# Turning part of q and x by DMA instead of on TensorE, with two batches of loads held behind these turns and batch 2's work scheduled four slots later

## Chip, cores, metric

One core of one Trainium2 chip. The metric is the device time of one execution in microseconds (us). Engine names are those of the profile: PE is TensorE, DVE is VectorE, ACT is ScalarE, POOL is GpSimd, SP is SyncE (it only issues DMA here; "SPq" is its queue).

## The reference, cut

```python
kv  = einsum('bhsd,bhse->bhde', k, v)             # 8 batches, 8 heads, 576 rows, 64 wide
out = einsum('bhsd,bhde->bhse', q, kv)
out = out / sqrt(mean(out*out, -1) + 1e-6) * g_norm
x   = out.transpose(0, 2, 1, 3).reshape(8, 576, 512)
xn  = (x - mean) / sqrt(var + 1e-6) * g_ln
return x + relu(xn @ w_ch1) @ w_ch2               # 512 -> 2048 -> 512
```

## The kernel before

The two large matrix products (the MLP) form one stream on TensorE. Its unit here is the **slot**: one group of matmuls, 0.86 to 0.89 us. Each batch takes 32 slots, 16 for the first product (mm1) and 16 for the second (mm2): slots 32 and 48 start mm1 and mm2 of batch 1, 64 and 80 those of batch 2, slot 96 mm1 of batch 3. The attention of later batches is put between the slots by an agenda. `at(slot, fn)` runs fn, that is, emits its instructions, just before that slot. In this kernel batch 4's q had landed by 101.8 us (87.9 + 13.9), and DVE copied it only at 106.18, after the tile work emitted ahead of it; SP sent an x turn that was ready at 106.26 only at 110.22, behind a q turn.

```python
def load_batch(b, after=None):
    if after is not None:
        nc.gpsimd.tensor_copy(gate, after)   # L98: the loads are issued behind this one-element copy
    load(k_in[b % NB], k, b)                 # two buffers each of k, v, q
    load(v_in[b % NB], v, b)
    load(q_in[b % NB], q, b)
...
def turn_q_dma(b):
    nc.vector.tensor_copy(q_p ..., q_in[b % NB])              # L202, DVE
    nc.sync.dma_start_transpose(q_t ..., q_p ...)             # L204, SP, 20 blocks of 128x128
...
def kv_of(b):
    kv_ps = ps_m.tile(..., tag="misc")       # K^T V, L245; ps_m has ONE buffer
...
class Tile:                                  # 128 rows of x
    o()    # q times KV on PE (L270), into ps_out, two buffers
    sq()   # ACT      red()  # DVE
    y()    # DVE L302 x()    # DVE L321     xc()  # DVE L331
    def turn(self, on_pe):
        if on_pe:
            tp = ps_m.tile(..., tag="misc")                   # the same single buffer
            ... four PE transposes (L347), then an ACT copy (L349)
        else:
            nc.sync.dma_start_transpose(dst, self.xc_t)       # L351, SP, four blocks
...
def plan_tile(s, make, turn_at, on_pe):
    at(s, o, sq, red);  at(s + 2, y, x, xc);  at(s + 6, var);  at(turn_at, turn)
...
q_turns(23, 1)        # batch 1's q: five turns on PE (L170), slots 23 to 26.5
for j, s, tn in ((0, 24, 30), (1, 27, 34), (2, 31, 38), (3, 35, 42)):
    plan_tile(s, lambda j=j: main_tile(1, j), tn, True)
at(36, lambda: kv_of(2))
at(36.5, lambda: turn_q_dma(2))
for j, s, tn in ((0, 44, 50), (1, 48, 54), (2, 53, 61), (3, 58, 67)):
    plan_tile(s, lambda j=j: main_tile(2, j), tn, j > 1)      # two tiles turned by DMA, two on PE
plan_tile(62, lambda: rem_tile(1), 69, False)                 # the 64 rows left over of batches 0 and 1
for b in range(3, B):
    s = 32 * b
    at(47 if b == 3 else s - 60,
       lambda b=b: load_batch(b, qts[b - 1][:1, J, HP - 1, 127:]))
    d = -41 if b == 3 else -45
    at(s + d, lambda b=b: kv_of(b));  at(s + d + 1.7, lambda b=b: turn_q_dma(b))
    for j in range(J):
        o = s + d + (10 if b == 3 else 13) + 5 * j
        plan_tile(o, lambda b=b, j=j: main_tile(b, j), o + 6, False)
    if b % 2:
        plan_tile(s - 14, lambda b=b: rem_tile(b), s - 8, False)
```

Slot 96 (mm1 of batch 3) needs all four x tiles of batch 3 turned, and its neighbour in the stream needs batch 4's q turned. Both are DMA transposes on SP.

## Time and profile before

| | before |
|---|---|
| time, median of 3 runs | 290.87 us (290.82 to 290.95) |
| span of the profiled run | 289.2 us |
| granted TensorE clock | 1.00 |
| PE idle from 30 us to slot 96 | 0.9 us of 83.2 |

The page of the kernel before, parts 1, 2 and 4 (busy time and share of each engine; busy tenths and granted clock in 40 slices; the chain of work that ended last):

```profile
PE 279.8 (97%) x2289; PEld 158.9 (55%) x2315; DVE 149.8 (52%) x331; ACT 155.4 (54%) x338; POOL 40.9 (14%) x68
PE   7889999999999999999999999999999999999995
PEclk9999999999999999999999999999999999999999
PE 91%; DMA 2%; DVE 2%; ACT 2%; issue 1%; DVEq 0%; POOLq 0%
```

TensorE bounds the kernel: busy everywhere, full clock, and the chain of waits is almost all PE. So I took every stall put into its stream to lengthen the kernel.

The timeline of POOL's gate copies before (start, duration, engine, line, operation; in brackets the idle time ahead of it and what ended it), for the loads of batches 3 and 4:

```profile
61.90 0.18 POOL L98 COPY gate<-qt 1x1 bf16<-1x1 bf16 x1 [23.43 <-DMA qt<-q_p]
83.38 0.18 POOL L98 COPY gate<-qt 1x1 bf16<-1x1 bf16 x1 [16.93 <-DMA qt<-q_p]
```

So a batch's loads begin when the q turn of the batch before has landed: a late q turn makes the next batch's loads late, and so its K^T V and its q turn.

The timeline of the kernel before, selected lines of DVE, SP and PE near slot 96:

```profile
105.51 0.75 DVE L331 SCALAR_TENSOR_TENSOR xc<-x_blk,st_blk,g_ln_sb 128x512 bf16<-128x512 f32 x1
106.18 0.82 DVE L202 COPY q_p<-q_in 128x2560 bf16<-128x2560 bf16 x1
107.06 3.11 SPq L204 DMA_TRANSPOSE qt<-q_p  x1
110.22 1.26 SPq L351 DMA_TRANSPOSE xT_blk<-xc  x1
112.66 0.39 PE L270 MATMUL o_ps<-kv_pack,qt 128*128 128x128 bf16 x4
112.88 1.89 PE L412 MATMUL p<-xT_blk,w_sb 128*128 128x512 bf16 x8
```

Batch 4's q turn goes out at 107.06 and batch 3's last x turn behind it at 110.22. The latter took 2.5 us to land (tile view), so it landed at about 112.7, and slot 96 starts at 112.88 without a stall. There is about 0.2 us of slack. (The tile itself was ready at 106.26, so its turn stood 4.0 us behind the q turn here too, and cost nothing.)

### The profile page before, as it was taken

The numbers are of one execution on the slowest core, as the hardware profiler recorded it, in microseconds if no ns is written. First come the engines' busy times: TensorE is split into PE (matmuls) and PEld (weight loads), VectorE is DVE, ScalarE is ACT, GpSimd is POOL, SyncE is SP. The second block draws the span as 40 slices with busy tenths as digits, with TensorE's granted clock in tenths as the row PEclk, the third lists the DMA queues.
The fourth block names the chain that finished last, engine by engine and source line by source line (L and its number), as shares of the span: only waits on it lengthen the run. The fifth ranks groups of instructions, "written<-read, shape, count | busy, mean of one in ns | idle before, by whom it ended". The sixth has DMA issues, their size and how long they took to land.

```text
span 289.2 us, 5765 instructions
## 1 busy us (share of the span) xinstructions
PE 279.8 (97%) x2289; PEld 158.9 (55%) x2315; DVE 149.8 (52%) x331; ACT 155.4 (54%) x338; POOL 40.9 (14%) x68
## 2 busy tenths in 40 slices
PE   7889999999999999999999999999999999999995
PEld 3579755995569644445444444444444444444444
DVE  5774028838987783765366925762578300220022
ACT  3477854985469832882288418920894076016500
POOL 8522520031032003200410022000000000000000
PEclk9999999999999999999999999999999999999999
DMA  7999999569999929996997179937202510131033
GB/s 215 199 208 202 201 203 206 125 103 196 151 168 129 178 53 165 184 164 123 144 211 102 39 146 204 170 79 161 54 18 54 111 36 0 39 82 27 0 74 73
DMA packets 64890, 36.10 MB, mean 125 GB/s; under 512 B 32860, under 2 KB 59868, under 8 KB 64864
## 3 DMA queue, kind: packets, MB, share of 16 engines
q0 software_dynamic: 28528, 17.76, 46.0%
q1 hardware_dynamic: 35824, 17.25, 31.3%
q10 hardware_dynamic: 512, 0.72, 0.7%
q8 instruction: 18, 0.29, 0.4%
q14 instruction: 8, 0.07, 0.1%
HBM read 36.71 MB, written 9.44 MB: 160 GB/s over the span
## 4 chain that ended last, share of the span: by engine, by line
PE 91%; DMA 2%; DVE 2%; ACT 2%; issue 1%; DVEq 0%; POOLq 0%
PE p L428 43%; PE p L412 42%; PE o_ps L270 3%; DMA v_in<-in_v_dram 2%; PE kv_ps L245 2%; ACT m L415 1%; DVE x_blk L288 0%; DVE xc L546 0%; PE tp L347 0%; ACT sq L276 0%; ACT xT_blk L349 0%; PE tp L170 0%; ACT rms L307 0%; DVE ss L512 0%; PE tp L553 0%
## 5 line engine op out<-in xcount | busy, mean ns | idle before, releaser
L412 PE MATMUL p<-xT_blk,w_sb 128*128 128x128 bf16 (+2 forms) x1017 | 131.4, 285 | 0.8
L428 PE MATMUL p<-w_sb,m 128*128 128x512 bf16 (+2 forms) x590 | 126.8, 368 | 1.6 <-issue 1.0
L415 ACT ACTIVATE m<-p 128x512 bf16<-128x512 f32 x144 | 85.4, 596 | 43.9 <-PE p L412 41.8
L412 PEld LDWEIGHTS <-w_sb 128*128 128x128 bf16 x1024 | 78.6, 98 | 44.5 <-issue 1.1
L428 PEld LDWEIGHTS <-m 128*128 128x128 bf16 x608 | 56.8, 98 | 61.7
L433 DVE SCALAR_TENSOR_TENSOR o_sb<-p,rstd,x_blk 128x512 f32<-128x512 f32 (+2 forms) x38 | 27.3, 721 | 53.2 <-PE p L428 47.6
L276 ACT ACTIVATE sq<-o_ps 128x512 f32<-128x512 f32 x35 | 20.9, 596 | 42.1 <-PE o_ps L270 42.1
L297 DVE TENSOR_REDUCE ss<-sq 128x8 f32<-128x512 f32 x35 | 23.7, 678 | 11.4 <-ACT sq L276 11.4
L339 ACT ACTIVATE dev<-x_blk,st_blk 128x512 f32<-128x512 f32 x36 | 25.7, 714 | 4.6 <-DVE st_blk L325 4.4
L331 DVE SCALAR_TENSOR_TENSOR xc<-x_blk,st_blk,g_ln_sb 128x512 bf16<-128x512 f32 x34 | 25.6, 752 | 1.2
L302 DVE TENSOR_TENSOR y<-o_ps,inv 128x512 f32<-128x512 f32 x33 | 22.8, 692 | 3.0
L321 DVE SCALAR_TENSOR_TENSOR x_blk<-y,g_norm_sb 128x512 f32<-128x512 f32 x33 | 22.8, 692 | 1.1
L314 DVE RECIPROCAL inv<-rms 128x8 f32<-128x8 f32 x36 | 7.2, 201 | 24.8 <-ACT rms L307 24.8
L421 DVE RECIPROCAL rstd<-rstd 128x4 f32<-128x4 f32 x9 | 1.6, 174 | 34.7 <-ACT rstd L420 34.7
L98 POOL COPY gate<-qt 1x1 bf16<-1x1 bf16 x5 | 0.9, 176 | 113.2 <-DMA qt<-q_p 113.2
L307 ACT ACTIVATE rms<-ss,eps_sb 128x8 f32<-128x8 f32 x36 | 10.7, 297 | 8.0 <-DVE ss L297 7.7
L270 PEld LDWEIGHTS <-qt 128*128 128x128 bf16 (+1 forms) x156 | 10.2, 100 | 7.3 <-issue 1.7
L270 PE MATMUL o_ps<-kv_pack,qt 128*128 128x128 bf16 (+1 forms) x156 | 13.7, 220 | 0.1
L197 PE MATMUL p<-fill_sb 128*128 128x512 bf16 x26 | 7.8, 449 | 1.3 <-DVE eps_sb L137 1.2
L339 ACT ACTIVATION_READ_ACCUMULATOR dev<-x_blk,st_blk 128x1 f32 x36 | 6.9, 190 | 0.0
L248 ACT CAST kv_pack<-kv_ps 64x256 bf16<-64x256 f32 x7 | 2.6, 365 | 7.2 <-PE kv_ps L245 7.2
L245 PEld LDWEIGHTS <-k_in 128*64 128x64 bf16 x280 | 5.0, 112 | 2.6 <-issue 2.5
(79 smaller groups left out, 116.5 us busy)
## 6 DMA issues: line engine op xcount, KB each, us to landing
out_dram<-o_sb SPq DMA_DIRECT2D x70, 128.0 KB, 2.4
w_sb<-in_moe_w_ch_dram POOLq DMA_DIRECT2D x8, 512.0 KB, 14.0
k_in<-in_k_dram POOLq DMA_DIRECT2D x7, 320.0 KB, 5.8
v_in<-in_v_dram POOLq DMA_DIRECT2D x7, 320.0 KB, 10.2
q_in<-in_q_dram POOLq DMA_DIRECT2D x7, 320.0 KB, 13.0
q_in<-in_q_dram POOLq DMA_DIRECT2D x8, 256.0 KB, 13.3
k_in<-in_k_dram POOLq DMA_DIRECT2D x7, 256.0 KB, 7.4
v_in<-in_v_dram POOLq DMA_DIRECT2D x7, 256.0 KB, 11.0
```

The costliest lines, as they stand in the source:

```text
L245: nc.tensor.matmul(kv_ps[hh * D:hh * D + D, hp, :], lhsT=k_in[b % NB][:, h, j, :], rhs=v_in[b % NB][:, h, j, :], start=(j == 0), stop=(j = ...
L270: nc.tensor.matmul(flat[rows, hp * 128:(hp + 1) * 128], lhsT=lhsT_of(hp), rhs=kvp[:, hp, :], start=True, stop=True)
L276: nc.scalar.activation(self.sq_t, self.o_ps, func=AF.Square)
L297: nc.vector.tensor_reduce(self.ss, self.sq_t, axis=AX.X, op=ALU.add)
L302: nc.vector.tensor_mul(self.y_t, self.o_ps, self.inv().to_broadcast([128, H, D]))
L321: nc.vector.scalar_tensor_tensor(x_blk[:, ts].rearrange("p (h d) -> p h d", h=H), in0=self.y_t, scalar=1.0, in1=g_norm_sb.to_broadcast([12 ...
L331: nc.vector.scalar_tensor_tensor(self.xc_t, in0=x_blk[:, self.ts], scalar=st[:, 1, self.ts:self.ts + 1], in1=g_ln_sb, op0=ALU.add, op1=ALU ...
L339: nc.scalar.activation(dev, x_blk[:, ts], func=AF.Square, bias=st[:, 1, ts:ts + 1], accum_out=st[:, 2, ts:ts + 1])
L412: nc.tensor.matmul(p1[:, i, :], lhsT=w1_sb[:, kk, de * 128:(de + 1) * 128], rhs=blk[2][:, kk, sl], start=(kk == 0), stop=(kk == nK - 1))
L415: nc.scalar.activation(m1[:, de0:de0 + per, sl], p1, func=AF.Relu)
L428: nc.tensor.matmul(p2[:, c0:c1], lhsT=m1s[b][:, de, ts * 128:(ts + 1) * 128], rhs=w2_sb[:, de, c0:c1], start=(de == 0), stop=(de == nDe - 1))
L433: nc.vector.scalar_tensor_tensor(o_sb[:, c0:c1], in0=p2[:, c0:c1], scalar=rstds[b][:, ts:ts + 1], in1=blks[b][0][:, ts, c0:c1], op0=ALU.mu ...
```

## The change

Its intent is to take 20 transposes of 128x128 blocks off the engine that bounds: three of batch 1's five q turns (12 blocks) and two x tiles of batch 2 (8 blocks) go to DMA transposes on SP. So that these do not run beside loads, batch 2's loads are held behind batch 1's q turn, and batch 4's behind an x turn of batch 2 as well as batch 3's q turn. Since batch 2's loads come later, its work is moved on.

```diff
-    def load_batch(b, after=None):
-        if after is not None:
-            nc.gpsimd.tensor_copy(gate, after)
+    def load_batch(b, *after):
+        for element in after:
+            nc.gpsimd.tensor_copy(gate, element)
... (next_loads)
-        load_batch(2)
+        load_batch(2, qts[1][:1, J, HP - 1, 127:])
...
-    at(9.5, next_loads)
... (q_turns)
+            q_p = q_ps.pop(b)
+            nc.sync.dma_start_transpose(
+                qts[b][:, 2:].rearrange("p j hp t -> p (j hp) t"),
+                q_p[:, 2:].rearrange("p j h d -> p (j h d)"))
-        for i, j in enumerate((2, 3, 4)):
-            at(s + 1.5 + i, lambda j=j: turn_q(b, j, ps_m, "misc"))
-        at(s + 4, lambda: q_ps.pop(b))
...
+    at(24, next_loads)
...
-    at(36, lambda: kv_of(2))
-    at(36.5, lambda: turn_q_dma(2))
-    for j, s, tn in ((0, 44, 50), (1, 48, 54), (2, 53, 61), (3, 58, 67)):
-        plan_tile(s, lambda j=j: main_tile(2, j), tn, j > 1)
-    plan_tile(62, lambda: rem_tile(1), 69, False)
+    at(38.5, lambda: kv_of(2))
+    at(41.5, lambda: turn_q_dma(2))
+    for j, s, tn in ((0, 48, 54), (1, 52, 58), (2, 56, 62), (3, 60, 66)):
+        plan_tile(s, lambda j=j: main_tile(2, j), tn, False)
+    plan_tile(70, lambda: rem_tile(1), 76, False)
...
-           lambda b=b: load_batch(b, qts[b - 1][:1, J, HP - 1, 127:]))
-        d = -41 if b == 3 else -45
+           lambda b=b: load_batch(b, qts[b - 1][:1, J, HP - 1, 127:],
+                                  *([blks[2][2][:1, nK - 1, 511:]] if b == 4 else [])))
+        d = -39 if b == 3 else -45
```

All of batch 3's attention comes two slots later (d from -41 to -39).

## The prediction

> **What bounds it now.** TensorE. The page's first part has PE busy 279.8 of 289.2 us (97%), at a granted clock of full speed in every slice; the chain of waits is 91% PE (two matmul lines 43% and 42%). After 18 us the chain has almost no gap. Time falls only by PE work removed, and rises by stalls put into PE's stream.
>
> **What the change removes.** Twelve PE transposes of batch 1's q (three of five turns) and eight of batch 2's x (two of its tiles). In the chain a full turn of four costs 0.22 us and the half turn about 0.16: 0.6 + 0.44 = about 1.0 us of PE, all of it on the critical path. Five ACT copies go too; ACT is not the bound, so they save nothing by themselves.
>
> **What it adds.** One DMA transpose of 12 blocks and two more of 4. Twenty blocks take 3.2 us of SP issue and land after 5.1 us (DMA view). The copy of q ends at 38.2 us, so I expect the 12 blocks to land at 42.5 to 44.
>
> **What it moves.** Batch 2's loads, issued from 30.3 us before, now wait for that landing and start near 43 to 44.5. A batch's six loads need (batch 3, timeline and DMA view) 9.3 us from first issue until v has landed and 13.1 until q has. Then batch 2: v 53 to 55, wanted by PE near 55.3 (slot 38); q 57 to 59, wanted by DVE near 58.5. Its q turn lands at about 64.5 (61.9 before), wanted near 65.5. Margins under 2 us, no large stall.
>
> Batch 3's loads follow that landing: first issue about 65.0 (62.4 before). v lands at 74.3 to 74.8; PE wants it at about 73.9: a stall of 0.4 to 0.9 us. Its q turn should land near 84.2, just as wanted.
>
> Batch 2's last x turn goes out on SP behind batch 3's q turn (3.2 us) and stores, landing at about 88 to 90; PE wants it near 89. Batch 4's loads now wait for it: first issue about 88.5 to 90 (84.6 before). There [...] v needed 13 us: 101 to 103, wanted at about 100.5. That stall, 0 to 2.5 us, is the largest risk.
>
> [...] an x turn lands in 2.5 us undisturbed and in 10.4 beside batch 4's loads.
>
> **Sum.** -1.0 of PE work, +0.9 of new stalls in the middle of my estimates: 290.8 us, 8 in 10 between 289.4 and 292.6. Chances: faster by over 2% 0.01, within 2% 0.96, slower by over 2% 0.03.
>
> **What would show it.** PE busy falls by about 1 us. New PE idle time in front of the K^T V matmuls of batches 3 and 4 (waiting for v), none or under 0.5 us at batch 2. The gate copy ahead of batch 2's loads at 43 to 45 us, of batch 3's near 64.5, of batch 4's 88 to 90.
>
> **What would make it wrong.** If 12 blocks land by 42 and loads run as fast as batch 3's, no stall appears and the time is about 289.8. If batch 0's stores slow batch 2's loads by over 2 us, each later batch inherits the delay and the time passes 292.

The x turn's 2.5 and 10.4 us and v's 13 us are measured in the kernel before. The sum is -1.0 + 0.9 = -0.1 us, from 290.9 to 290.8.

## More of the kernel before

The windows view of the kernel before, from 30 us to 0.3 us past the start of slot 96 (length, then busy time and count of each engine, clock, DMA share, GB/s):

```profile
core 0: us, PE busy (x) PEld busy (x) DVE busy (x) ACT busy (x) POOL busy (x), PEclk, DMA share, GB/s
30.00:113.20 83.20, 82.29 (x897) 56.83 (x903) 54.38 (x117) 52.90 (x123) 13.15 (x23) 1.00 1.06 156
```

## The result, and the profile after

| | before | after |
|---|---|---|
| time, median of 4 runs | 290.91 us (290.82 to 291.21) | 301.71 us (300.64 to 302.92) |
| ratio after/before | | 1.037 (1.033 to 1.041): slower |
| span of the profiled run | 289.2 us | 298.5 us |
| PE idle from 30 us to slot 96 | 0.9 us | 9.25 us |

A ratio is the mean time of one kernel's fast runs over that of the other's of the same rounds, so it is not quite the ratio of the medians. The result lies far outside the predicted range. The profiled run of after was its fastest, with a mean granted clock of 0.998; its other runs had 0.994 to 1.000.

The page of the kernel after, the same parts:

```profile
PE 283.1 (95%) x2295; PEld 158.5 (53%) x2295; DVE 150.0 (50%) x331; ACT 153.7 (51%) x333; POOL 41.2 (14%) x70
PE   8999999799789898799999999999999999999994
PEclk9999999999999999999999999999999999999999
PE 65%; DMA 11%; DVE 9%; issue 6%; ACT 4%; SPq 2%; POOL 1%; DVEq 0%; POOLq 0%; ACTq 0%
```

The PE row has dents (7 and 8) from the eighth slice to the nineteenth and none later, and the chain has moved from PE to DMA, DVE and waits. PE's busy time did not fall, but 18 mm2 matmuls (590 against 608) and 7 of mm1 (1017 against 1024) are missing from the records of before, so the busy sums of the two pages are not compared. That the 20 transposes are gone shows in the weight loads, which are complete: PEld x2315 before, x2295 after.

The windows view of the kernel after, from 30 us to 0.3 us past the start of slot 96:

```profile
30.00:122.25 92.25, 83.00 (x886) 56.13 (x884) 55.67 (x118) 51.70 (x118) 15.20 (x27) 1.00 0.94 150
```

The stretch is 9.05 us longer and PE is idle for 8.34 us more of it, at full clock. The two differ by 0.7 us, about what missing records and modelled ends allow. So nearly all of the loss is PE waiting, before slot 96. Where TensorE stood at the slot starts (PE timeline of both):

| start of | slot 48 | slot 64 | slot 80 | slot 96 | end of span |
|---|---|---|---|---|---|
| before | 66.64 | 82.22 | 97.75 | 112.88 | 289.2 |
| after | 67.80 | 84.78 | 102.26 | 121.93 | 298.5 |
| difference | +1.2 | +2.6 | +4.5 | +9.05 | +9.3 |

The last column adds almost nothing: from batch 3's MLP on the two kernels run alike in these two profiled runs. Half of the loss falls between slots 80 and 96.

The PE timeline of the kernel after, its waits of over half a microsecond up to slot 96:

```profile
56.81 0.82 PE L245 MATMUL kv_ps<-v_in,k_in 128*64 128x64 bf16 x40 [1.50 <-ACT xT_blk L349]
...
67.57 0.40 PE L270 MATMUL o_ps<-kv_pack,qt 128*128 128x128 bf16 x4 [0.67 <-DMA qt<-q_p]
...
77.75 0.82 PE L245 MATMUL kv_ps<-v_in,k_in 128*64 128x64 bf16 x40 [1.57 <-DMA v_in<-in_v_dram]
...
88.80 0.40 PE L270 MATMUL o_ps<-kv_pack,qt 128*128 128x128 bf16 x4 [1.24 <-ACT m L415]
...
99.65 2.78 PE L412 MATMUL p<-xT_blk,w_sb 128*128 128x256 bf16 x24 [0.74 <-ACT m L415]
...
104.89 0.41 PE L270 MATMUL o_ps<-kv_pack,qt 128*64 128x128 bf16 x8 [0.52 <-DVE y L302]
...
115.58 3.61 PE L428 MATMUL p<-w_sb,m 128*128 128x512 bf16 x16 [0.68 <-DVE o_sb L433]
...
119.81 0.40 PE L270 MATMUL o_ps<-kv_pack,qt 128*128 128x128 bf16 x4 [0.62 <-DMA qt<-q_p]
...
121.93 4.49 PE L412 MATMUL p<-xT_blk,w_sb 128*128 128x512 bf16 x20 [1.72 <-DMA xT_blk<-xc]
```

They sum to 9.3 us (1.50 + 0.67 + 1.57 + 1.24 + 0.74 + 0.52 + 0.68 + 0.62 + 1.72), nine waits and no large one. Only the third is a load (v of batch 3), and none is v of batch 4, which I had called the largest risk. The first is a wait for a PSUM buffer: batch 2's v had landed at 54.8, but K^T V of batch 2 and the PE turn of batch 1's third x tile now fall in the same slot 38 and share the single "misc" buffer, so that K^T V waits for ACT's copy of the turn. The wait at 88.80 is batch 3's q turn, whose landing released the gate at 88.88: the profile puts PE's wait down to ACT, but the weight load of the same matmul waited 1.52 us for DMA qt<-q_p. The wait at 99.65 is for ScalarE's eviction, which stood in program order behind a small activation (L307 at 98.81) that had waited 1.21 us for VectorE's sum (L297).

POOL's gates of the kernel after, for the loads of batches 2, 3 and 4 (two gates for batch 4):

```profile
43.74 0.18 POOL L98 COPY gate<-qt 1x1 bf16<-1x1 bf16 x1 [13.55 <-DMA qt<-q_p]
67.64 0.18 POOL L98 COPY gate<-qt 1x1 bf16<-1x1 bf16 x1 [19.32 <-DMA qt<-q_p]
88.88 0.18 POOL L98 COPY gate<-qt 1x1 bf16<-1x1 bf16 x1 [16.63 <-DMA qt<-q_p]
93.54 0.18 POOL L98 COPY gate<-xT_blk 1x1 bf16<-1x1 bf16 x1 [4.49 <-DMA xT_blk<-xc]
```

The first is where I put it (43 to 44.5). The second, predicted at 64.5, came at 67.64: VectorE waited 1.44 us for q of batch 2 and copied it at 59.98, and the turn, issued at 60.83, took 6.7 us to land instead of 5.1. The last, predicted for 88 to 90, came at 93.54.

The timeline of the kernel after near slot 96, selected lines of DVE and SP, to be held against the six lines of before:

```profile
110.84 0.75 DVE L331 SCALAR_TENSOR_TENSOR xc<-x_blk,st_blk,g_ln_sb 128x512 bf16<-128x512 f32 x1 [0.30 <-DVE st_blk L325]
...
113.39 0.75 DVE L331 SCALAR_TENSOR_TENSOR xc<-x_blk,st_blk,g_ln_sb 128x512 bf16<-128x512 f32 x1
114.05 0.82 DVE L202 COPY q_p<-q_in 128x2560 bf16<-128x2560 bf16 x1
114.94 3.11 SPq L204 DMA_TRANSPOSE qt<-q_p  x1
118.14 0.54 SPq L446 DMA_DIRECT2D out_dram<-o_sb  x1
118.74 0.59 SPq L447 DMA_DIRECT2D out_dram<-o_sb  x1
119.38 2.60 SPq L351 DMA_TRANSPOSE xT_blk<-xc  x2
```

Batch 3's last x tile was ready at about 111.6 (110.84 + 0.75) but its turn went out at 119.38, behind batch 4's q turn and two stores. It is this turn for which slot 96 waits at 121.93. The q turn itself is late because VectorE came to its copy at 114.05 (106.18 before), behind the work of two x tiles: batch 3's last tile now shares slots 82 and 84 with the remainder tile of batches 2 and 3.

### The profile page after: what moved, and what is told of

Read it like the earlier page. It is cut to its first block, busy times and chain, and to the rows that moved or that the text cites. A ratio compares the mean times of both kernels' runs of the same rounds, so it can differ in the third digit from the quotient of the medians.

```text
span 298.5 us, 5751 instructions
## 1 busy us (share of the span) xinstructions
PE 283.1 (95%) x2295; PEld 158.5 (53%) x2295; DVE 150.0 (50%) x331; ACT 153.7 (51%) x333; POOL 41.2 (14%) x70
## 4 chain that ended last, share of the span: by engine, by line
PE 65%; DMA 11%; DVE 9%; issue 6%; ACT 4%; SPq 2%; POOL 1%; DVEq 0%; POOLq 0%; ACTq 0%
PE p L428 31%; PE p L412 31%; DMA q_in<-in_q_dram 4%; DMA qt<-q_p 2%; PE o_ps L270 2%; DMA out_dram<-o_sb 2%; DMA gn_row<-in_g_norm_dram 2%; ACT m L415 2%; DVE y L302 1%; DVE ss L297 1%; DVE x_blk L321 1%; SPq L204 1%; PE kv_ps L245 1%; ACT rms L307 1%; DVE o_sb L433 1%
## 5 line engine op out<-in xcount | busy, mean ns | idle before, releaser
L428 PE MATMUL p<-w_sb,m 128*128 128x512 bf16 (+2 forms) x608 | 128.9, 368 | 0.7 <-DVE o_sb L433 0.7
L297 DVE TENSOR_REDUCE ss<-sq 128x8 f32<-128x512 f32 x35 | 23.7, 678 | 11.9 <-ACT sq L276 11.9
L331 DVE SCALAR_TENSOR_TENSOR xc<-x_blk,st_blk,g_ln_sb 128x512 bf16<-128x512 f32 x34 | 25.6, 752 | 1.5 <-DVE st_blk L325 0.3
L307 ACT ACTIVATE rms<-ss,eps_sb 128x8 f32<-128x8 f32 x36 | 10.6, 297 | 11.4 <-DVE ss L297 11.3
L197 PE MATMUL p<-fill_sb 128*128 128x512 bf16 x27 | 9.4, 508 | 1.2 <-DVE eps_sb L137 1.2
L245 PE MATMUL kv_ps<-v_in,k_in 128*64 128x64 bf16 x280 | 5.8, 197 | 3.1 <-DMA v_in<-in_v_dram 1.6
```

Of the source, the lines that this page charges most:

```text
L245: nc.tensor.matmul(kv_ps[hh * D:hh * D + D, hp, :], lhsT=k_in[b % NB][:, h, j, :], rhs=v_in[b % NB][:, h, j, :], start=(j == 0), stop=(j = ...
L297: nc.vector.tensor_reduce(self.ss, self.sq_t, axis=AX.X, op=ALU.add)
L331: nc.vector.scalar_tensor_tensor(self.xc_t, in0=x_blk[:, self.ts], scalar=st[:, 1, self.ts:self.ts + 1], in1=g_ln_sb, op0=ALU.add, op1=ALU ...
L428: nc.tensor.matmul(p2[:, c0:c1], lhsT=m1s[b][:, de, ts * 128:(ts + 1) * 128], rhs=w2_sb[:, de, c0:c1], start=(de == 0), stop=(de == nDe - 1))
```

## The experiments

Eighteen kernels ran; all gave correct results. Four timed runs of each (five of the best one).

| label | what | median us | ratio (95%) |
|---|---|---|---|
| r1_no_hold_2 | after, batch 2's loads not held | 302.55 | 1.039 (1.036 to 1.042) |
| r2_no_hold_4 | after, batch 4's second gate away | 309.57 | 1.063 (1.058 to 1.067) |
| r3_hold_2_alone | before, batch 2's loads held | 297.29 | 1.021 (1.016 to 1.027) |
| r4_turns_alone | before, both kinds of DMA turn | 299.69 | 1.028 (1.022 to 1.034) |
| r5_x_turns_alone | before, x turns by DMA | 297.66 | 1.023 (1.022 to 1.025) |
| r6_q_turn_alone | before, q turns by DMA | 291.95 | 1.004 (1.002 to 1.005) |
| r7_x_on_pe | after, x turns back on PE, no second gate | 302.79 | 1.042 (1.039 to 1.045) |
| r8_move_alone | before, only the later slots | 301.61 | 1.036 (1.034 to 1.038) |
| s1_tiles_late_alone | before, batch 2's tiles later | 292.43 | 1.005 (1.004 to 1.007) |
| s2_rem_and_b3_late | before, remainder and batch 3 later | 297.82 | 1.023 (1.021 to 1.025) |
| s3_rem_early | after, remainder tile early | 301.56 | 1.038 (1.034 to 1.041) |
| s5_part | before, 8 q blocks and one x tile by DMA | 290.45 | 0.9987 (0.9974 to 0.9999) |
| t1_b3_late_alone | before, batch 3 two slots later | 296.99 | 1.021 (1.018 to 1.023) |
| t2_rem_late_alone | before, remainder tile later | 293.11 | 1.007 (1.006 to 1.009) |
| t3_b3_tiles_back | after, batch 3's last three tiles at their old slots | 299.15 | 1.028 (1.023 to 1.033) |
| t4_b2_move_alone | before, batch 2 later | 297.54 | 1.024 (1.021 to 1.027) |
| u1_b3_late_turn_first | t1 with the x turn ahead on SP | 292.10 | 1.004 (1.002 to 1.005) |
| u2_after_turn_first | after with the x turn ahead on SP | 300.67 | 1.034 (1.030 to 1.039) |

Before of the same rounds was between 290.88 and 291.01 throughout. Executions of one kernel differ by up to 3.9 us (r4) once PE waits long, and the longer ones mostly have the lower mean clock: r8 took 300.51 us at 1.000 and 301.57 to 301.85 at 0.993 to 0.994, t3 297.74 and 298.03 at 1.000, 300.27 and 300.58 at 0.994. Differences of a microsecond between two such kernels therefore mean little by themselves. The theories at the start were: the holds make loads late (what my prediction feared); the DMA turns themselves land late; the moved slots cost it.

### The holds taken away from the kernel after

```diff
  r1_no_hold_2
-        load_batch(2, qts[1][:1, J, HP - 1, 127:])
+        load_batch(2)
-    at(24, next_loads)
+    at(9.5, next_loads)
  r2_no_hold_4
-                                  *([blks[2][2][:1, nK - 1, 511:]] if b == 4 else [])))
+                                  ))
```

> The changed kernel with batch 2's loads issued at once again (near 30 us), all else as changed. Theory A (the hold puts batch 2's loads, and through the gate copies those of 3 and 4, on one serial chain of load, copy, turn that starts too late): most of the 10.8 us comes back, 290 to 293 us, the gate ahead of batch 3's loads falls from 67.6 to under 64 us, and the idle time of TensorE between 60 and 105 us falls from about 8 us to under 3. Theory B (the second hold of batch 4 behind the x turn is what costs): 299 us or more. Theory C (moving batch 2's work four slots on collides with other work on PSUM and the in-order engines): 298 us or more. Theory D (a turn by DMA beside loads is too slow): 299 us or more, since turns and loads now overlap more.

> The changed kernel without the second gate copy of batch 4. Its loads start at the landing of batch 3's q turn, 88.9 us, instead of 93.5. Theory A: 4.7 us of the chain go, and the stalls after 107 us (about 3 us) with them, nothing before: 297 to 299 us. Theory B: 293 us or less. Theory C: no change, over 300 us.

Neither helped. Without batch 2's hold the time stayed at 302.55 us. The issue of batch 1's q turn, now beside loads, took 3.25 us instead of 1.54 and PE waited 1.99 us for its landing. That wait replaced what the hold had cost, and the two waits of the kernel after for batch 2's q turn (0.67) and batch 3's v (1.57) were gone; the others were there (0.24 to 2.37 us each). So the hold of batch 2's loads alone is not the cause. Without batch 4's second gate the kernel lost another 8 us. The PE timeline of that run, at mm1 of batch 2:

```profile
101.15 6.91 PE L412 MATMUL p<-xT_blk,w_sb 128*128 128x256 bf16 x40 [5.92 <-DMA xT_blk<-xc]
```

An x turn landing beside batch 4's loads made PE wait 5.92 us in one piece. Given the DMA turns, this hold is needed.

### Each part put into the kernel before

r3 adds the hold of batch 2's loads (on an element that the PE turns write last, at slot 27.5), r4 both kinds of DMA turn, r5 and r6 one kind each, r8 only the changed slot numbers.

```diff
  r3_hold_2_alone
-        load_batch(2)
+        load_batch(2, qts[1][:1, J, HP - 1, 63:64])
-    at(9.5, next_loads)
+    at(27.5, next_loads)
  r4_turns_alone: the two lines of r5 and r6 together
  r5_x_turns_alone
-        plan_tile(s, lambda j=j: main_tile(2, j), tn, j > 1)
+        plan_tile(s, lambda j=j: main_tile(2, j), tn, False)
  r6_q_turn_alone: the q_turns part of the change
  r8_move_alone
-    at(36, lambda: kv_of(2)) ... turn_q_dma(2) at 36.5, tiles ((0, 44, 50), (1, 48, 54), (2, 53, 61), (3, 58, 67))
+    at(38.5, lambda: kv_of(2)) ... at 41.5, tiles ((0, 48, 54), (1, 52, 58), (2, 56, 62), (3, 60, 66))
-    plan_tile(62, lambda: rem_tile(1), 69, False)
+    plan_tile(70, lambda: rem_tile(1), 76, False)
-        d = -41 if b == 3 else -45
+        d = -39 if b == 3 else -45
```

> The kernel before with nothing but the hold: batch 2's loads wait until batch 1's last q turn (on TensorE) is copied, about 44.6 us. Theory A: the loss appears without any DMA turn, move or second hold: 296 us or more, with TensorE waiting for v of batch 2 at slot 36 and for later q turns. Theories B, C and D: within 2 us of the kernel before, 291 to 293.

> The kernel before with nothing but the turns by DMA (three fifths of batch 1's q, the last two x tiles of batch 2), no hold, no move. Theory A: the 1.0 us of TensorE work comes off, less a small stall where a turn runs beside batch 2's loads: 289.8 to 291.5 us. Theory D: turns land 8 us or more after issue and stall TensorE at the third tile of batch 1 (near 48 us) and at batch 2's third tile, 293 us or more.

> The kernel before with only the last two x turns of batch 2 by DMA. Theory E (a turn by DMA that goes out beside a batch's loads lands 7 to 12 us after issue, and TensorE stands until it lands[...]): the last x turn meets batch 4's loads, TensorE stands 3 to 4 us at slot 72 and then runs slow for 3 to 5 us: 294 to 297 us, mean clock below 0.99. Theory F (the loss is the later start of the loads, on the serial chain from one batch's q turn to the next batch's loads): nothing moves here, so 290 to 291 us.

> The kernel before with only batch 1's q turn (12 blocks) by DMA. Theory E: it meets batch 2's loads, lands near 50 us, TensorE stands 2 us at the third tile of batch 1 and runs slow after it: 293 to 295 us, with no further stall over 1 us later. Theory F: 290 to 291 us.

> The kernel before with only batch 2's work moved four slots on (and the slots of the remainder tile and of batch 3 with it), no DMA turn, no hold. Theory E: no turn meets loads, so under 292 us. Theory F: the gate of batch 3's loads falls later by 2.5 to 3.5 us (61.9 to about 65), batch 3's q turn with it, and TensorE waits for v of batch 3 and for its q turn: 293 to 295 us. Theory C (a new collision on the single PSUM buffer that x turns and K^T V share: both now stand in slot 38): a stall of 1.5 us at K^T V of batch 2, waiting for ACT's copy, in this run as in the changed kernel.

Every part alone costs time: the hold +6.3 us, the x turns +6.8, the q turn +1.1, both turns +8.7. The move alone costs +10.7, as much as the whole change (+10.8). It has no DMA turn and no hold beyond those of before. So the later slots suffice to lose everything, and with the slots moved the holds and the turns add nothing on balance. That the slots are also necessary is not shown: the change with its holds and turns but with the old slots was not run, and r3 and r4 lose 6.3 and 8.7 us in the old slots.

The PE timeline and then two windows of r4 (both turns in the old slots, no holds):

```profile
50.09 0.40 PE L270 MATMUL o_ps<-kv_pack,qt 128*128 128x128 bf16 x4 [2.08 <-DMA qt<-q_p]
...
96.36 5.30 PE L412 MATMUL p<-xT_blk,w_sb 128*128 128x256 bf16 x24 [3.49 <-DMA xT_blk<-xc]
```

```profile
52.00:54.00 2.00, 2.00 (x22) 2.00 (x21) 0.63 (x1) 0.41 (x1) 0.00 (x0) 0.50 1.23 302
98.00:100.00 2.00, 2.00 (x12) 1.39 (x10) 0.00 (x0) 0.60 (x2) 0.00 (x0) 0.50 1.35 183
```

Two things are to be seen. The turns beside loads land late, 2.08 and 3.49 us after PE wants them. And the granted clock (third column from the right) was 0.50 after each wait: the 24 matmuls after the second took 5.30 us where 24 such matmuls take 2.78 in the kernel after. r5 shows the same with a wait of 4.02 us (0.50 from 94 to 98); r6, with a wait of 1.72, kept the full clock (1.00 from 46 to 54). A wait of about two microseconds thus cost more than its length in some runs and not in others. The PE timelines of r8 and then of r7 at slot 96 show the same wait of 2.44 us, with 6.18 us for the 20 matmuls after it in the first (mean clock of the run 0.994) and 4.49 in the second (0.999):

```profile
122.12 6.18 PE L412 MATMUL p<-xT_blk,w_sb 128*128 128x512 bf16 x20 [2.44 <-DMA xT_blk<-xc]
```

```profile
122.79 4.49 PE L412 MATMUL p<-xT_blk,w_sb 128*128 128x512 bf16 x20 [2.44 <-DMA xT_blk<-xc]
```

The SP queue on batch 1's q turn, in the kernel after (loads held) and then in r4 (loads running):

```profile
38.58 1.54 SPq L612 DMA_TRANSPOSE qt<-q_p  x1
```

```profile
38.24 3.35 SPq L613 DMA_TRANSPOSE qt<-q_p  x1
```

The 12 blocks landed at 43.7 in the first, 5.1 us after issue, and at about 50 in the second, 11.8 us after (PE, which waited for them, went on at 50.09).

r7 asked the opposite question, whether the kernel after recovers if the x turns go back to PE (and the second gate goes, as nothing needs it then):

```diff
  r7_x_on_pe
-        plan_tile(s, lambda j=j: main_tile(2, j), tn, False)
+        plan_tile(s, lambda j=j: main_tile(2, j), tn, j > 1)
  and the second gate of batch 4 away
```

> The changed kernel with batch 2's last two x turns back on TensorE and so without the second hold (batch 4's loads start at the landing of batch 3's q turn). Theory E says the x turn and its hold cost only what the hold delays: the gate of batch 4 falls from 93.5 to about 89 us and the stalls after 98 us (4.3 us in sum) shrink to under 2: 297 to 299 us. Theory F says that stalls before 90 us (5 us) remain in full, which E agrees with for the hold of batch 2. If the x turns were the main part, 294 us or less.

It did not: 302.79 us, with the same late waits (0.74, 0.51, 0.42, 0.61 and 2.44 us). In the kernel after the x turns by DMA are not the cause.

### Which part of the move

```diff
  s1_tiles_late_alone     tiles of batch 2 to ((0, 48, 54), (1, 52, 58), (2, 56, 62), (3, 60, 66))
  s2_rem_and_b3_late      plan_tile(70, rem_tile(1), 76) and d = -39
  s3_rem_early            the kernel after with plan_tile(42, rem_tile(1), 49)
  t1_b3_late_alone        d = -39, nothing else
  t2_rem_late_alone       plan_tile(70, rem_tile(1), 76), nothing else
  t4_b2_move_alone        kv_of(2) at 38.5, turn_q_dma(2) at 41.5, and s1's tiles
```

> The kernel before with only the four tiles of batch 2 moved to the changed kernel's slots (48, 52, 56, 60); K^T V and the q turn of batch 2, the remainder tile and batch 3 stay. Theory G (the move empties VectorE at 60 to 68 us, where it did the first tile or two of batch 2, and this work then queues up behind other work until slot 96, so x of batch 2 and 3 and q_p come late): gates of batches 3 and 4 stay near 62 and 83 us, but TensorE still waits for xc, for evictions and for batch 3's last x: 293 to 297 us. Theory F (the later loads of batch 3 are what costs): no gate moves, so under 292 us.

> The kernel before with only the remainder tile of batches 0 and 1 (slot 62 to 70) and batch 3's work (two slots later) moved. Theory G: VectorE's 3.3 us for the remainder tile now fall among batch 3's tiles, so batch 3's last x and q_p of batch 4 come late: TensorE waits 1 to 2 us at slot 96: 291.5 to 293 us. Theory F: the loads are unchanged, within 0.5 us of the kernel before.

> The changed kernel with the remainder tile of batches 0 and 1 at slot 42 (its turn at 49), that is in VectorE's hole of 60 to 66 us, instead of slot 70. Theory G: 3.3 us leave VectorE's queue between 92 and 114 us, and the stalls of TensorE after 98 us (4.3 us in sum in the changed kernel) fall to under 1.5 us: 297.5 to 299.5 us. Theory F: the chain of loads is unchanged, so no gain, over 300.5 us.

> The kernel before with only batch 3's work two slots later. Theory I (batch 3's last tile now falls into slots 82 and 84 with the remainder tile of batches 2 and 3 and behind the eviction of slot 83; both tiles stand before batch 4's q copy on VectorE, and that q turn stands before batch 3's last x turn on SP, which slot 96 needs at once): most of the 6.9 us, 295.5 to 298 us, nearly all lost between slots 80 and 96, with a wait of 2 to 2.5 us for the last x turn and a lower clock after it. Theory G (VectorE's load from the late remainder tile of batches 0 and 1): within 1.5 us of the kernel before.

> The kernel before with only the remainder tile of batches 0 and 1 at slot 70 instead of 62. Theory I: within 1 us of the kernel before. Theory G: 294 us or more, with VectorE late at slot 96.

> The kernel before with only batch 2's K^T V, q turn and tiles at the changed slots; remainder tile and batch 3 as before. Theory I with F: the gate of batch 3's loads falls from 62 to about 67 us, its q turn lands near 88 us, wanted at slot 65 (about 84): TensorE has lost 4 to 5.5 us by slot 80 and no more after it: 294.5 to 296.5 us. If K^T V and q turn cost nothing beyond the tiles (1.5 us), 292.5 us.

Measured against before: s1 +1.5 us, s2 +6.9, t1 +6.1, t2 +2.2, t4 +6.7. s3, which takes the remainder tile of batches 0 and 1 out of the crowded stretch, left the kernel after where it was (301.56 us). That does not clear VectorE: in the profiled run of s3 (its slowest, 303.82 us) the waits at 99.65 and 104.89 are gone and slot 80 starts 1.1 us earlier (101.14), but then PE waits for v of batch 4, which in the kernel after it did not:

```profile
106.63 1.28 PE L245 MATMUL kv_ps<-v_in,k_in 128*64 128x64 bf16 x40 [2.28 <-DMA v_in<-in_v_dram]
```

My expectation for t2 (under 1 us) was missed; that the remainder tile costs 2.2 us by itself I have not followed further. The times of r6, r7, r8, s1, s2, t3 and t4 also fell outside what any theory in their texts allowed, r8 (301.61, where at most 295 was said) and s2 (+6.9, where at most about 2 was said) by the most.

Two separate losses are left. One is batch 2's move (t4). Its delay at slot 80 is already 6.0 us, at slot 96 6.2, so it falls early. The POOL timeline of t4, batch 3's gate:

```profile
67.23 0.18 POOL L98 COPY gate<-qt 1x1 bf16<-1x1 bf16 x1 [28.18 <-DMA qt<-q_p]
```

It stands at 61.90 in before. The q copy of batch 2, moved from slot 36.5 to 41.5, lets all of batch 3's loads start 5.3 us later (the turn is issued 3.6 us later, at 60.47, and takes 6.7 us to land instead of 5.0), though batch 2's own loads are as early as ever. PE then waits 1.42 us for the PSUM buffer at batch 2's K^T V, as in the kernel after (1.50) and in r8 (1.42), and 2.18 us for v of batch 3.

The other is batch 3's two slots (t1). It loses nothing until slot 80 and 3.9 us at slot 96 (116.82), and the remaining 2.7 of its profiled run's 6.6 in the slow matmuls just after. The PE timeline and the SP queue of t1:

```profile
116.82 7.17 PE L412 MATMUL p<-xT_blk,w_sb 128*128 128x512 bf16 x20 [2.61 <-DMA xT_blk<-xc]
```

```profile
108.91 3.07 SPq L204 DMA_TRANSPOSE qt<-q_p  x1
112.07 0.54 SPq L446 DMA_DIRECT2D out_dram<-o_sb  x1
112.67 0.59 SPq L447 DMA_DIRECT2D out_dram<-o_sb  x1
113.31 2.85 SPq L351 DMA_TRANSPOSE xT_blk<-xc  x2
```

This is the pattern of the kernel after, made by two slots alone. The last x tile was ready at 105.6 (VectorE ended it at 104.81 + 0.75), its turn went out at 113.31, and PE waited 2.61 us; the 20 matmuls then took 7.17 us, where those of the kernel after take 4.49, at a granted clock of 0.50 until 122.

### The order on SP, tested

u1 is t1 with one number more: batch 3's last x turn is emitted at slot 84.65, just ahead of batch 4's q turn, instead of at slot 88. u2 is the same in the kernel after. t3 is the kernel after with the second to fourth of batch 3's tiles back at their old slots (the first stays at 67, two slots late).

```diff
  u1_b3_late_turn_first (on t1), u2_after_turn_first (on after)
-            plan_tile(o, lambda b=b, j=j: main_tile(b, j), o + 6, False)
+            plan_tile(o, lambda b=b, j=j: main_tile(b, j),
+                      84.65 if (b, j) == (3, 3) else o + 6, False)
  t3_b3_tiles_back (on after)
-            o = s + d + (10 if b == 3 else 13) + 5 * j
+            o = (67, 70, 75, 80)[j] if b == 3 else s + d + 13 + 5 * j
```

> The run with only batch 3 two slots late (296.99 us), with one turn issued earlier on SP: batch 3's last x turn ahead of batch 4's q turn instead of behind it. VectorE's order is the same up to the q copy. Theory I: the x turn goes out near 105.6 us and lands before 112, TensorE no longer waits for it at slot 96 and keeps its clock; what stays is the wait for batch 4's q turn (0.65 us, now some 1.3 us later at most): 291.5 to 293.5 us. If VectorE's late q copy is what counts and not the order on SP: 295.5 us or more.

> The changed kernel with the same one reordering: batch 3's last x turn on SP ahead of batch 4's q turn. Its wait of 1.7 us at slot 96 should go; but here batch 4's q copy stands at 114.05 us and its q turn lands at 119.8, so TensorE then waits for that, up to 1.3 us longer: slot 96 falls from 121.9 to about 121, 300 to 301.2 us, with the delay already there at slot 80 (4.5 us) untouched. If the order on SP is the main part here too, 297.5 us or less.

> The changed kernel with batch 3's second to fourth tile back in the slots they had before (70, 75, 80); its first tile, K^T V and q turn stay as changed. Theory I: batch 3's last x turn is out of the way of the remainder tile, the delay at slot 96 falls from 9 us to 4.5 to 6 us, which is what the late loads of batches 2 and 3 have cost by slot 80: 295.5 to 298 us. If slot 96 is held up by batch 4's late loads just as much (their gate stands at 93.5 us), no gain: over 300 us.

u1 came to 292.10 us: 4.9 of t1's 6.1 us were the order on SP, the slow matmuls after the wait included. Its SP queue:

```profile
105.53 1.19 SPq L351 DMA_TRANSPOSE xT_blk<-xc  x1
...
108.85 3.06 SPq L204 DMA_TRANSPOSE qt<-q_p  x1
```

The x turn goes out when its tile is ready, 7.8 us earlier, and the q turn goes out no later than in t1 (108.85 and 108.91). PE no longer waits for x, and the 20 matmuls at slot 96 take 4.48 us (mean clock of the run 0.999). In t1 the q turn, which went out at 108.91, after VectorE's copy (108.02 + 0.82), kept a finished tile behind it in SP's queue. Of the 7.8 us in t1, 3.4 passed before the q turn went out and 4.4 went into issuing it and two stores.

In the kernel after the same reordering was worth 1.0 us (u2, slot 96 at 120.97 instead of 121.93; the intervals of the two ratios overlap), since there the q turn of batch 4 and the earlier waits bind as well. t3, which moves three tiles back, won 2.6 us at slot 96 (delay 6.4 instead of 9.05) and came to 299.15 us. So in the kernel after this place is worth 1.0 to 2.6 us by what was tried, and the rest is upstream.

### A smaller version of the change

s5 turns only two of the three q turns (8 blocks) and one x tile of batch 2 by DMA, with no hold and no move, so that each turn has time to land.

```diff
  s5_part
-        for i, j in enumerate((2, 3, 4)):
-            at(s + 1.5 + i, lambda j=j: turn_q(b, j, ps_m, "misc"))
+            nc.sync.dma_start_transpose(          # in start(), after the first two turns
+                qts[b][:, 3:].rearrange("p j hp t -> p (j hp) t"),
+                q_ps[b][:, 3:].rearrange("p j h d -> p (j h d)"))
+        at(s + 1.5, lambda: turn_q(b, 2, ps_m, "misc"))
-        plan_tile(s, lambda j=j: main_tile(2, j), tn, j > 1)
+        plan_tile(s, lambda j=j: main_tile(2, j), tn, j == 3)
```

> A smaller change that should beat both: the kernel before with only the last 8 blocks of batch 1's q and only the third x tile of batch 2 by DMA, since those are wanted late enough: TensorE loses 0.22 + 0.16 + 0.22 = 0.6 us of turns and should not wait (the q blocks land near 49.5 us and are wanted at 52.5; the x turn goes out before batch 4's loads and lands near 86, wanted at 89.5): 290.1 to 290.5 us. If turns beside loads are worse than thought, over 291 us.

It is the only version below before: 290.45 against 290.89 us over five rounds, ratio 0.9987 (0.9974 to 0.9999). Its one new wait is 0.24 us for batch 3's q turn; PE stood 0.86 us earlier at slot 48 and 0.9 us earlier at slot 96, and the span ended 0.6 us earlier.

## Why the prediction was wrong

**PE work removed, -1.0 us: right in kind, somewhat small.** With only the 12 q blocks gone, PE reached the same matmuls at 46.76 in the kernel after and at 47.76 in before: 1.0 us, where I had put 0.6 on these and 0.4 on the x turns.

**"Margins under 2 us, no large stall" for batch 2: the loads right, the stall wrong.** The gate came at 43.74 as said and v landed at 54.8 (said: 53 to 55). But PE stood still for 1.50 us there, for the shared PSUM buffer. The check was made for the load alone, though two users of a one-buffer pool had been moved into one slot.

**"Its q turn lands at about 64.5": 67.6.** The copy started at 59.98 (I had 58.5) and the turn took 6.7 us instead of 5.1. All of batch 3 inherited this: v with a wait of 1.57 us (said: 0.4 to 0.9), the q turn with 1.24 (said: just as wanted).

**"That stall, 0 to 2.5 us, is the largest risk" (batch 4's v): hidden, not absent.** Its gate came at 93.54, 3.5 us past the predicted range, and v landed at about 104.8 (said: 101 to 103). There was no wait only because PE, held up before, reached this K^T V at 106.20 and not at 100.5. In s3, where PE came at 104.35 and v landed at 106.5, it waited 2.28 us, and in t3 0.87. That the stall did not show in the kernel after is luck.

**The step that failed is the sum: "+0.9 of new stalls".** Nine waits with 9.3 us stood in its place. I had followed the loads through the moved slots, and left out three other things: PSUM buffers (the first wait, 1.50 us, and the one at 104.89), the program order of VectorE and ScalarE (the q copy at 114.05 behind two tiles, the evictions behind 99.65), and SP's program order at slot 96 (the last x turn of batch 3, 7.8 us behind its tile), though I had followed that order for batch 2's last x turn. Before had about 0.2 us of slack at slot 96; a change that moved batch 3 two slots and left batch 4's q turn where it was had to be checked there first. The hint was in VectorE's timeline of before near slot 96: batch 4's q had landed by 101.8 us, and its copy at 106.18 comes after the tile work emitted ahead of it (the last of it, L331, at 105.51).

**Where the +10.8 us come from, as far as the runs settle it.** r8 shows that the slots alone are enough for the whole loss. t4 and t1 show two parts, +6.7 and +6.1. They do not add up with the others: r3, r5, r6, t4, t1 and t2 sum to 29 us (6.3 + 6.8 + 1.1 + 6.7 + 6.1 + 2.2). The parts use up the same slack, and undoing one of them leaves the others binding; that reading is argued from the sums, and it is what r1, r7, s3 and u2 look like.

**What stays open.** Why batch 2's q turn took 6.6 to 6.7 us to land in the kernel after, r2, r7, r8, t3, t4 and u2 (6.0 in s3), and 4.9 to 5.0 in the other runs. Other traffic does not explain the end of it: in the kernel after the DMA engines moved nothing from 66.0 on, and the landing came at 67.6. How the loss between slots 48 and 96 splits exactly in the kernel after. Its times spread over 2.3 us (300.64 to 302.92), when before spreads over 0.4: the two longest had a mean clock of 0.994, the profiled one 0.998, but that of 301.22 had 1.000, so the clock is a part of it and not all. The trace shown here is of the fastest, which lost 9.3 us of span, not the median's 10.8.

## What to carry to other kernels

In a kernel whose TensorE stream has no slack, moving work by a few slots is itself a change with a cost (r8: +10.7 us): write down for each moved piece its place in the order of every queue that kept its order here (VectorE, SP) and every shared PSUM buffer (a wait of 1.50 us in the kernel after), and check each against the slot that needs the result. On a queue that issues DMA, put the transfer that is ready first: in t1 a q turn that waited for a late copy held a finished x turn behind it, which went out 7.8 us later than in u1. And when the costs of single parts add up to far more than the whole, suspect one shared slack (argued here from sums, not shown), and test by reordering in place instead of undoing more parts.

## What these runs show of the clock and of turns beside loads

- After some waits of PE the granted clock was lower, or the matmuls were slower: 1.76 us (s3, with 0.63 us of waiting just before: the next 20 matmuls took 5.89 us instead of 4.49), 2.00 (r2: 40 matmuls took 0.94 us instead of 0.82, clock 0.7 in that slice of the page), 2.08 (r4: 0.50), 2.28 (s3: 0.53), 2.44 (r8: 6.18 us instead of 4.49), 2.61 (t1: 0.50). Others were not followed by it: 1.72 (r6 and the kernel after: clock 1.00), 1.99 (r1, r3: 1.00), 2.18 (t4: 40 matmuls in 0.82 us), 2.37 (r1: 20 in 4.49), 2.44 (r7: 20 in 4.49). So the length of one wait does not decide it in these runs, and no limit can be read from them.
- 12 blocks landed after 5.1 us with loads held and after 11.8 us beside them (r4), an x turn after 2.5 us and, beside batch 4's loads, after 10.4 us (both in the kernel before). Why they land later there is not shown.
- An independent transfer behind a waiting one on SP went out 7.8 us later, waiting and issue together, which was 4.9 us of the kernel's time (t1 against u1).
